# A gated mix of linear attention and a bilinear feed-forward block: the turn between two pairs of token chunks laid out step by step

## The chip, the core and the metric

The kernel runs on one core of a Trainium2 chip. It is judged by the device time of one execution in microseconds (us). The engines are named as in the profile: PE is the matrix engine (PEld its weight loads), DVE the vector engine, ACT the scalar engine, POOL the GpSimd engine, SP the engine that only issues DMAs here. Each takes its own instructions in the order in which the program was written (every compute helper of this kernel pins that order) and waits for the others by semaphores.

## What is computed

Input x has 2048 tokens of 512 features. The output mixes two branches per token, with g a sigmoid of a weighted sum of the token:

```python
g = _sigmoid((x * gate_w).sum(-1, keepdims=True))
a = _A_ref(x, A_wqkv, A_wo)            # linear attention, 32 heads of 16
b = _B_ref(x, B_w_gate, B_w_up, B_w_down)   # ((x W) * (x V)) W2, F = 1792
return g * a + (1 - g) * b
```

In the attention, phi(t) = t + 1 where t > 0, else exp(t), plus 1e-6; kv = sum of phi(k) v, z = sum of phi(k), and o = (phi(q) kv) / (phi(q) z + 1e-6), then o times wo. Nothing in it depends on the order of tokens.

## The kernel before

**Precision.** Every large product is done with operands split in two float32r parts, hi (a rounded copy, written by ACT, names ending in h) and lo (the rest, written by DVE with a subtraction, names ending in l), in three matmuls of 128x128 by 128x512: hi hi, hi lo, lo hi (`mm3`). So each operand that PE reads costs one ACT and one DVE instruction first: `hh`/`hl` for h = (xW)(xV), `oh`/`ol` for the attention's o, `wch`/`wcl` and `dh`/`dl` for weights, `xah`/`xal` and the like for x.

**Stages.** A first stage makes kv, z and the gates. Then the tokens are worked off in two *pairs* of two 512-token chunks each (c = 0 and 1). A pair has 16 *units*: two of kind q (q for half of the heads) and 14 of kind f (one 128-wide piece of W and V). A unit multiplies 2x2 blocks in the manner of Strassen: seven products, six matmuls each, in the order `UNIT`, accumulated in the PSUM banks bY, bX, bR and bS, with DVE's bR, t and bS between them: bR (in step 1) must be there for the product of step 3, t (step 3) for that of step 5, bS (step 4) for that of step 6. Each of the seven steps is a *slot*. Slots are numbered through, 7 per unit, 112 per pair, so that pair 0's last unit is slots 105 to 111. In a slot the program issues, in this order: the product, what is due from the slot before (`evacuate`), what is written for that slot in a table (`later(slot, fn)`), the unit's own step, and a *job* of three matmuls of the down projection, which lags by a group of two units and is also made of seven products; its sums are held in SBUF tiles M (`macc[i, d]`), the one of product 1 in PSUM (`pM`).

**The turn.** After a pair's last unit, `turn(pair)` closes the pair. 48 *pieces* of three matmuls make the outputs: 8 outputs (four row blocks d for c=1, then four for c=0) of 6 pieces, four with the operands `oh`, `ol` and two with those of h's last four blocks (`"12"`, `"22"` for c=1, `"11"`, `"21"` for c=0). When an output's pieces are done, DVE adds the bank to the M tile that holds that block of the down projection (`M<-M,pdn`), and it is stored. Pair 1 has all 48 pieces in its turn; of pair 0 30 are in the turn and 18 in the first 18 slots of pair 1. Until an output's sum, DVE has to

- gate h's last blocks with 1 - g (`c<-c,omg`) and split them (`plain`, through `hi_lo`);
- add M tiles to each other to get the blocks C12, C22, C21 and C11 (`add`, rows `M<-M` or `M<-M,pM`; 12 of them in the turn) and scale them with 1 - g (`scale`, rows `M<-M,omg`; 8 of them). In `ends` they stand as a list: sums of a block, then scales, two blocks after each other; `turn` takes two of the list per piece in the first five steps and one in each later;
- split o (`o_split`), c=1 in the last unit, c=0 in steps 18 to 21 of the turn;
- for pair 0, split pair 1's x (`x_split`, seven splits of 128x1024), whose parts are loaded in the last unit.

**q scaling.** In `attention`, the normaliser's reciprocal is stored and read back broadcast (`norm`, a DMA `rb<-den` on SP) and multiplied into q (`scale`, DVE `phq<-phq,rb`), four times for each of the two q units (j), three slots apart. `ZAT[j]` holds the slots, counted from that unit; its last number is the first `norm`, and `scale` follows six slots later.

**Buffers.** All 128x512 work tiles come from one pool of 45 (`get`, `put`) handed out in the order in which they were given back; the new owner waits for the last reader of the old.

Of the kernel before, what the change touches and what calls it, by code (L numbers as in the profile page):

```python
# [10 lines left out]
ALU = mybir.AluOpType  # L11
# [14 lines left out]
NPAIR = NC // 2  # L26
# [5 lines left out]
NG = NF // 2  # L32
# [4 lines left out]
UNIT = (2, 3, 4, 1, 5, 6, 7)  # L37
# [5 lines left out]
def gated_mix(ctx: ExitStack, tc, xt, xp, x, wqkv, wq, wq_add, wo, wgu, wgu_add, wdn, wdn_add, wdl, gate_w, out):  # L43
# [12 lines left out]
    def act(dst, src, func=AF.Copy, **kw):  # L56
        pin(nc.scalar.activation(dst, src, func, **kw))  # L57

    def tt(dst, a, b, op):
        pin(nc.vector.tensor_tensor(dst, a, b, op=op))  # L60
# [19 lines left out]
    def dma(dst, src):  # L80
        tc.keep_in_program_order(nc.sync.dma_start(dst, src))
# [42 lines left out]
    units = len(order)  # L124
# [61 lines left out]
    def get(name):  # L186
        k = spare.pop(0)
        w = p2.tile([P, CH], F32R, tag=f"w{k}", name=name)
        held[id(w)] = (k, w)
        return w  # L190

    def put(*ws):
        for w in ws:
            spare.append(held.pop(id(w))[0])

    def f32(w):
        return w.bitcast(F32)
# [12 lines left out]
    def later(slot, fn):  # L210
        at.setdefault(slot, []).append(fn)

    def do(table, slot):
        for fn in table.pop(slot, []):
            fn()
# [23 lines left out]
    for t in range(2 * CH // P):  # L239
        c, i = divmod(t, CH // P)  # L240
# [11 lines left out]
    for k in range(KT):  # L252
        raw = f32(raw_of[k])
        a = get("xlead")
# [151 lines left out]
    def gate():  # L406

        act(gcol, scol, AF.Exp, scale=-1.0)
        pin(nc.vector.tensor_scalar_add(gcol, gcol, 1.0))
        pin(nc.vector.reciprocal(gcol, gcol))  # L410
        pin(nc.vector.tensor_scalar(ocol, gcol, -1.0, 1.0, op0=ALU.mult, op1=ALU.add))
        turned = get("turned")
        rows = f32(turned)[:, 0:2 * NT]
        pin(nc.vector.transpose(rows, both))
        for a in range(0, P, 2 * NT):
            dma(gates[:, a:a + 2 * NT], rows[a:a + 2 * NT])
        put(gw)
        later(now_slot[0] + 8, lambda: put(turned))
# [18 lines left out]
    def hi_lo(src, keep, hi_at, lo_at, when):  # L437

        two = []

        def hi():
            two.append(get("hh"))
            act(two[0], f32(src()))

        def lo():
            two.append(get("hl"))
            tt(two[1], f32(src()), f32(two[0]), ALU.subtract)
            if not keep:
                put(src())

        when(hi_at, hi)
        when(lo_at, lo)
        return two
# [8 lines left out]
    def d_load(g):  # L462
        if g < NPAIR * NG:
            draw[g] = p2.tile([P, 7, 2 * P], F32, tag="dr", name="dr")
            if g % NG < NG - 1:
                dma(draw[g][:, 0:3], wdn[g % NG])
            else:
                dma(draw[g][:, 0:4], wdl)

    def d_add(g):  # L470
        if g < NPAIR * NG and g % NG < NG - 1:
            copies(draw[g])
            dma_add(draw[g][:, 2:7], wdn_add[g % NG])

    def d_high(g, part):
        a, b = (PLAIN if g % NG == NG - 1 else DRAW)[part]
        dcs[g, part] = [p2.tile([P, b - a, 2 * P], F32R, tag=f"d{part}{v}", name=f"d{v}", bufs=1 + part // 2)
                        for v in "hl"]
        act(dcs[g, part][0], draw[g][:, a:b])

    def d_low(g, part):
        a, b = (PLAIN if g % NG == NG - 1 else DRAW)[part]
        h, l = dcs[g, part]
        tt(l, draw[g][:, a:b], h.bitcast(F32), ALU.subtract)

    macc = {}
    half = {1: [0, 1, 2, 3], 0: [2, 3, 0, 1]}

    class Group:
# [44 lines left out]
        def when(self, off, fn):  # L534
            if off >= 14 and self.last:
                tail.setdefault((self.pair, off), []).append(fn)
            else:
                later(self.T + off, fn)

        def plain(self):  # L540

            g, pair, when, B = self.g, self.pair, self.when, self.B
            self.rows, self.ends = {}, []

            def row(c):
                self.rows[c] = get("omg")
                there = gates[NT:2 * NT].rearrange("(n t) p -> n (t p)", n=NC)[2 * pair + c:2 * pair + c + 1]
                dma(f32(self.rows[c]), there[:, None, :].to_broadcast([1, P, CH]))

            def gate(key, c):  # L550
                tt(f32(B[key]), f32(B[key]), f32(self.rows[c]), ALU.mult)

            for c in range(2):
                when(3, lambda c=c: row(c))
            for key, c, off in (("12", 1, 6), ("11", 0, 7), ("22", 1, 13), ("21", 0, 14)):
                when(off, lambda key=key, c=c: gate(key, c))
                self.ops[key] = hi_lo(lambda key=key: B[key], False, off + 1, off + 2, when)
            for part, off in (2, 4), (1, 8):
                when(off - 1, lambda part=part: d_high(g, part))
                when(off + 1, lambda part=part: d_low(g, part))  # L560
            when(11, lambda: d_load(g + 1))
            when(14, lambda: d_add(g + 1))

            def add(a, b, d, op, free):
                m = macc[b, d]
                tt(f32(macc[a, d]), f32(macc[a, d]), m if b == STAYS else f32(m), op)
                if free and b != STAYS:
                    put(macc.pop((b, d)))

            for off, a, b in (2, 6, 2), (6, 7, 5):  # L570
                for d in range(2):
                    when(off + d, lambda a=a, b=b, d=d: add(a, b, d, ALU.subtract, False))

            def scale(d, c):
                w = c_tile(d, c)
                tt(f32(w), f32(w), f32(self.rows[c]), ALU.mult)
                if d == half[c][-1]:
                    put(self.rows[c])

            scales = [lambda d=d, c=c: scale(d, c) for c in (1, 0) for d in half[c]]  # L580
            adds = [[lambda d=d, a=a, b=b: add(a, b, d, ALU.add, (a, b) in ((6, 3), (7, 1), (7, 4)))
                     for a, b in some for d in range(2)]
                    for some in (((5, 3),), ((6, 1), (6, 3)), ((2, 4),), ((7, 1), (7, 4)))]
            self.ends = []
            for n in range(4):
                self.ends += adds[n] + scales[2 * n:2 * n + 2]

        def seed(self, i, d):
            if not self.first and i != STAYS:
# [31 lines left out]
        def job_of(self, off):  # L621
            k = off - 11
            return (DOWN[k // 2], k % 2) if 0 <= k < 14 else None

    groups = [Group(g) for g in range(NPAIR * NG)]

    def at_slot(slot):
# [126 lines left out]
    def x_split(i):  # L754
        hi, lo = xc[i]
        act(hi, lo.bitcast(F32))
        tt(lo, lo.bitcast(F32), hi.bitcast(F32), ALU.subtract)
# [70 lines left out]
                    rows[pair, c][:, None, :].to_broadcast([2, 2 * HB, P]))  # L828

    phs = {}  # L830
    ZAT = ((15, (21, 23, 24), 26, 28), (24, (31, 33, 35), 37, 40))
    QORDER = [(1, 0), (0, 1), (1, 1), (0, 0)]

    def attention(pair, j, n):
# [55 lines left out]
        for (r, c), s in zip(QORDER, (8, 8, 10, 13) if j == 0 else (8, 9, 10, 13)):  # L890
            later(T + s, lambda r=r, c=c: z_part(r, c))
            later(T + s + 5, lambda: put(zs.pop(0)))
        loads, adds, rec, first = ZAT[j]
        for e in range(4):
# [12 lines left out]
    def o_split(b, c):  # L907
        hi, lo, o = get("oh"), get("ol"), phs.pop((b, c))
        act(hi, f32(o))
        tt(lo, f32(o), f32(hi), ALU.subtract)  # L910
        put(o)
        os_[b, c] = [hi, lo]
# [3 lines left out]
    def pieces(k):  # L916
        for fn in queue[:k]:
            fn()
        del queue[:k]
# [3 lines left out]
    def c_tile(d, c):  # L923
        return macc[CAT[d // 2, c], d % 2]
# [34 lines left out]

    def turn(pair):  # L960

        gr = groups[pair * NG + NG - 1]
        ends_jobs(pair)
        ready = []
        for k in range(TURN[pair]):
            pieces(1)
            do(tail, (pair, 14 + k))
            do(tail, (pair, 14 + k, "x"))
            for fn in gr.ends[:2 if k < 5 else 1]:
                fn()  # L970
            del gr.ends[:2 if k < 5 else 1]
            for fn in ready:
                fn()
            ready = waiting[:]
            waiting.clear()
        waiting.extend(ready)

    TURN = (30, 48)
    for k in range(18):
        FILL[7 * units + k] = 1  # L980
    for i, off in zip(UNIT, (36, 38, 40, 41, 42, 43)):
        tail.setdefault((0, off, "x"), []).append(lambda i=i: x_split(i))
    later(7 * units + 1, lambda: x_split(7))
    for p in range(NPAIR):
        for k, off in enumerate((32, 33, 34, 35)):
            tail.setdefault((p, off, "x"), []).append(lambda k=k: o_split(k, 0))

    for p in range(NPAIR):
        last = 7 * (units * (p + 1) - 1)
        for k, s in enumerate((0, 2, 4, 5)):  # L990
            later(last + s, lambda k=k: o_split(k, 1))
    later(14, g2_load)
    later(15, g_evac)
# [15 lines left out]
    for n, (pair, kind, m) in enumerate(order):  # L1009
        unit(n, attention(pair, m, n) if kind == "q" else None)  # L1010
        if (n + 1) % units == 0:
            turn(pair)
# [59 lines left out]
```

## Time and profile before

| | us |
|---|---|
| median of 3 runs (lowest to highest) | 604.53 (603.42 to 605.12) |
| profiled execution | 603.9 |
| its span | 602.2 |
| DVE busy, ACT busy | 499.0, 408.9 |
| DMA busy, mean of 16 engines, by the three busy queues | 33.4%, 29.2%, 0.2% of the span |
| last matmul's start, last DVE instruction's start | 597.63, 598.06 |

The span is the time from the first to the last instruction of the profiled execution; 1.7 us lie around it. A row of the timeline reads: start, duration, engine, line, operation, output<-inputs, shapes, count, and in brackets the engine's idle time before and what ended it. Lines are those of the kernel, and most of the instructions come from one of four helpers (L51 matmuls, L57 ACT, L60 and L63 DVE), so that they are told apart by their tiles. A wait row reads: engine, tile and line that waited, what it waited for, us in total, number of times, longest.

### The profile page before, as it was taken

To read this page: it belongs to the slowest core of one execution; us is meant where nothing else is said; L and a number is where in the kernel's file an instruction comes from. 1 tells how busy PE (TensorE), PEld (TensorE's weight loads), DVE (VectorE), ACT (ScalarE), POOL (GpSimd) and SP (SyncE) were. 2 spreads that over 40 slices of the span, in tenths; PEclk is the share of its full clock that TensorE was granted. 3 is DMA by queue.
4 is the path that set the end of the run, shared out by engine and by line. 5 is a ranking of instruction groups with operands and counts; after the bars stand their busy time and mean duration, and the time that the engine had idled before them with its cause. 6 is when DMAs were issued, how large, how long until landed. Compare 5 with 4: busy or idle time off the path is not lost.

```text
span 602.2 us, 7746 instructions
## 1 busy us (share of the span) xinstructions
PE 588.0 (98%) x2579; PEld 480.1 (80%) x2579; DVE 499.0 (83%) x809; ACT 408.9 (68%) x734; POOL 61.2 (10%) x79
## 2 busy tenths in 40 slices
PE   8999999999999999999998899999999999999997
PEld 6888888888778888888877688887888888888775
DVE  6869967776998999888989956969999989799881
ACT  3858857668877877777763754888686878776300
POOL 0041000010011212021000200201010101000000
PEclk9999999999999999999999999999999999999999
DMA  8589566695684989787686157847855656340011
GB/s 305 202 180 302 129 207 153 136 261 125 151 217 114 198 212 225 183 202 182 164 227 202 70 123 192 172 138 189 202 121 117 167 112 134 78 100 14 0 71 70
DMA packets 44185, 95.55 MB, mean 159 GB/s; under 512 B 4305, under 2 KB 13521, under 8 KB 44113
## 3 DMA queue, kind: packets, MB, share of 16 engines
q0 software_dynamic: 9856, 36.18, 33.4%
q1 hardware_dynamic: 34144, 58.62, 29.2%
q8 instruction: 20, 0.33, 0.2%
q10 hardware_dynamic: 144, 0.26, 0.1%
q14 instruction: 21, 0.16, 0.1%
HBM read 83.76 MB, written 12.34 MB: 160 GB/s over the span
## 4 chain that ended last, share of the span: by engine, by line
PE 82%; DVE 10%; ACT 4%; DMA 2%; issue 2%; DVEq 0%; ACTq 0%
PE pdn L51 20%; PE bR L51 13%; PE bY L51 13%; PE bX L51 12%; PE pk L51 7%; PE gt L51 7%; PE bS L51 6%; DVE M L60 5%; PE pM L51 2%; DMA dr<-in_wdn 2%; DVE c L60 1%; DVE ol L60 1%; DVE wcl L60 1%; PE pkv L51 1%; ACT wch L57 1%
## 5 line engine op out<-in xcount | busy, mean ns | idle before, releaser
L60 DVE TENSOR_TENSOR wcl<-wr,wch 128x512 fp32r<-128x512 f32 (+1 forms) x96 | 74.2, 774 | 2.7 <-ACT wch L57 2.7
L51 PE MATMUL pdn<-hl,dh 128*128 128x512 f32 x176 | 68.7, 390 | 2.6 <-DVE hl L60 2.6
L60 DVE TENSOR_TENSOR M<-M,pdn 128x512 f32<-128x512 f32 x76 | 51.9, 683 | 21.8 <-PE pdn L51 21.8
L51 PE MATMUL pdn<-hh,dh 128*128 128x512 f32 x176 | 68.6, 390 | 0.0
L51 PE MATMUL pdn<-hh,dl 128*128 128x512 f32 x176 | 68.5, 389 | 0.0
L57 ACT ACTIVATE wch<-wr 128x512 fp32r<-128x512 f32 (+1 forms) x96 | 66.8, 699 | 0.0
L57 ACT ACTIVATE M<-pdn 128x512 f32<-128x512 f32 x84 | 50.3, 599 | 15.5 <-PE pdn L51 12.6
L57 ACT ACTIVATE hh<-c 128x512 fp32r<-128x512 f32 x56 | 35.2, 629 | 31.5 <-DVE c L60 31.4
L84 POOL DMA_DIRECT2D wr<-in_wgu_add x28 | 24.2, 865 | 296.3 <-ACT wr L57 156.2
L51 PE MATMUL bX<-xbh,wch 128*128 128x512 f32 x128 | 49.8, 389 | 0.0
L51 PE MATMUL bX<-xbh,wcl 128*128 128x512 f32 x128 | 49.8, 389 | 0.0
L51 PE MATMUL bX<-xbl,wch 128*128 128x512 f32 x128 | 49.8, 389 | 0.0
L51 PEld LDWEIGHTS pdn<-hl,dh 128*128 128x128 f32 x176 | 33.0, 188 | 10.1 <-DVE hl L60 3.4
L60 DVE TENSOR_TENSOR hl<-c,hh 128x512 fp32r<-128x512 f32 x56 | 38.5, 687 | 1.5 <-ACT hh L57 1.4
L51 PEld LDWEIGHTS pdn<-hh,dh 128*128 128x128 f32 x176 | 33.0, 188 | 7.2 <-ACT pdn L57 0.3
L51 PEld LDWEIGHTS pdn<-hh,dl 128*128 128x128 f32 x176 | 33.0, 188 | 6.9
L57 ACT ACTIVATE c<-bX 128x512 f32<-128x512 f32 x28 | 16.8, 601 | 30.4 <-DVE bS L60 30.4
L57 ACT ACTIVATE wr<-wr 128x512 f32<-128x512 f32 x64 | 36.7, 625 | 0.8 <-DMA wr<-in_wgu 0.8
L57 ACT ACTIVATE pdn<-M 128x512 f32<-128x512 f32 x60 | 35.5, 592 | 0.0
L57 ACT ACTIVATE m<-bY 128x512 f32<-128x512 f32 x32 | 19.0, 594 | 19.5 <-PE bY L51 17.7
L60 DVE TENSOR_TENSOR dl<-dr,dh 128x512 fp32r<-128x512 f32 (+1 forms) x40 | 29.6, 766 | 1.9 <-ACT dh L57 1.8
L60 DVE TENSOR_TENSOR t<-bR,c 128x512 f32<-128x512 f32 x32 | 22.0, 686 | 10.3 <-PE bR L51 9.4
(186 smaller groups left out, 1592.2 us busy)
## 6 DMA issues: line engine op xcount, KB each, us to landing
wr<-in_wgu_add POOLq DMA_DIRECT2D x28, 640.0 KB, 6.9
wr<-in_wgu SPq DMA_DIRECT2D x28, 384.0 KB
dr<-in_wdn_add POOLq DMA_DIRECT2D x12, 640.0 KB, 8.5
dr<-in_wdn SPq DMA_DIRECT2D x12, 384.0 KB
xraw<-in_x SPq DMA_DIRECT2D x16, 256.0 KB
terms<-zq SPq DMA_DIRECT2D x16, 256.0 KB
zt<-terms SPq DMA_DIRECT2D x16, 256.0 KB
rb<-den SPq DMA_DIRECT2D x16, 256.0 KB
```

The source lines that it names most:

```text
L51: tc.keep_in_program_order(nc.tensor.matmul(*args, **kw))
L57: pin(nc.scalar.activation(dst, src, func, **kw))
L60: pin(nc.vector.tensor_tensor(dst, a, b, op=op))
L84: tc.keep_in_program_order(nc.gpsimd.dma_start(dst, src, accum_op=ALU.add))
```

## The change

- h's last blocks `"22"` and `"21"` are split one step earlier: their hi parts in the same step as their gates (13 and 14, counted as offsets of the last group; the turn begins at 14), and by the order in which the steps were entered, both stand ahead of the M sums.
- The list `ends` is gone. Each sum and scale has an offset of its own (`steps`): sum and scale of a block alternate, and each block's come shortly ahead of its output sum. For pair 0, offsets of 44 and more, which are the six instructions of C11 (two sums and a scale for either half), go into slots 3, 4, 6 and 7 of pair 1. For pair 1 all stay in the turn.
- Four of the seven x splits (for the products 1, 5, 6, 7, `UNIT[3:]`) go to slots 0, 1, 2 and 4 of pair 1; before, three of them were in the turn and that of 7 in slot 1. Each stands two or three slots ahead of its product.
- The o splits of c=1 move from steps 0, 2, 4, 5 of the last unit to -3, -1, 0, 2 (the first two into the unit before).
- The `norm` of the first q unit starts at its slot 52 and not 28, so the loads stand at 52, 55, 58, 61 and the scales at 58, 61, 64, 67.

```diff
@@ plain
-            for key, c, off in (("12", 1, 6), ("11", 0, 7), ("22", 1, 13), ("21", 0, 14)):
+            for key, c, off in (("12", 1, 6), ("11", 0, 7)):
                 when(off, lambda key=key, c=c: gate(key, c))
                 self.ops[key] = hi_lo(lambda key=key: B[key], False, off + 1, off + 2, when)
+            when(13, lambda: gate("22", 1))
+            self.ops["22"] = hi_lo(lambda: B["22"], False, 13, 14, when)
+            when(14, lambda: gate("21", 0))
+            self.ops["21"] = hi_lo(lambda: B["21"], False, 14, 15, when)
...
-            scales = [lambda d=d, c=c: scale(d, c) for c in (1, 0) for d in half[c]]
-            adds = [[lambda d=d, a=a, b=b: add(a, b, d, ALU.add, (a, b) in ((6, 3), (7, 1), (7, 4)))
-                     for a, b in some for d in range(2)]
-                    for some in (((5, 3),), ((6, 1), (6, 3)), ((2, 4),), ((7, 1), (7, 4)))]
-            self.ends = []
-            for n in range(4):
-                self.ends += adds[n] + scales[2 * n:2 * n + 2]
+            def steps(off, *fns):
+                for k, fn in enumerate(fns):
+                    if pair == NPAIR - 1 or off + k < 14 + TURN[0]:
+                        when(min(off + k, 13 + TURN[pair]), fn)
+                    else:
+                        later(7 * units * (pair + 1) + (off + k - 14 - TURN[0]) // 2, fn)
+
+            for d in range(2):
+                steps(15 + 2 * d, lambda d=d: add(5, 3, d, ALU.add, False), lambda d=d: scale(d, 1))
+            for d in range(2):
+                steps(20 + 3 * d, lambda d=d: add(6, 1, d, ALU.add, False), lambda d=d: add(6, 3, d, ALU.add, True),
+                      lambda d=d: scale(2 + d, 1))
+            for d in range(2):
+                steps(39 + 3 * d, lambda d=d: add(2, 4, d, ALU.add, False), lambda d=d: scale(2 + d, 0))
+            for d in range(2):
+                steps(50 + 6 * d, lambda d=d: add(7, 1, d, ALU.add, False), lambda d=d: add(7, 4, d, ALU.add, True),
+                      lambda d=d: scale(d, 0))
@@ attention
-    ZAT = ((15, (21, 23, 24), 26, 28), (24, (31, 33, 35), 37, 40))
+    ZAT = ((15, (21, 23, 24), 26, 52), (24, (31, 33, 35), 37, 40))
@@ turn
-            for fn in gr.ends[:2 if k < 5 else 1]:
-                fn()
-            del gr.ends[:2 if k < 5 else 1]
@@
-    for i, off in zip(UNIT, (36, 38, 40, 41, 42, 43)):
+    for i, off in zip(UNIT, (36, 38, 40)):
         tail.setdefault((0, off, "x"), []).append(lambda i=i: x_split(i))
-    later(7 * units + 1, lambda: x_split(7))
+    for i, s in zip(UNIT[3:], (0, 1, 2, 4)):
+        later(7 * units + s, lambda i=i: x_split(i))
...
-        for k, s in enumerate((0, 2, 4, 5)):
+        for k, s in enumerate((-3, -1, 0, 2)):
             later(last + s, lambda k=k: o_split(k, 1))
```

PE's instructions and their order are the same in both kernels. Three places on DVE show what moves. The first is the end of pair 0's last unit and the start of its turn; `c` are the blocks of h, `wcl` next unit's weights, `t` and `bS` the unit's own steps. Before:

```order
L60 TENSOR_TENSOR t<-bR,c_3147 128x512
L60 TENSOR_TENSOR ol<-phq,oh 128x512
L60 TENSOR_TENSOR wcl<-wr,wch 128x512
L60 TENSOR_TENSOR bS<-t,bX 128x512
L60 TENSOR_TENSOR ol<-phq,oh 128x512
L60 TENSOR_TENSOR wcl<-wr,wch 128x512
L60 TENSOR_TENSOR c_3189<-bR,c_3189 128x512
L60 TENSOR_TENSOR c_3189<-c_3189,omg 128x512
L60 TENSOR_TENSOR c_3147<-bS,c_3147 128x512
L60 TENSOR_TENSOR c_3147<-c_3147,omg 128x512
L60 TENSOR_TENSOR M<-M 128x512 x2
L60 TENSOR_TENSOR hl<-c_3189,hh 128x512
```

And of the change:

```order
L60 TENSOR_TENSOR t<-bR,c_3155 128x512
L60 TENSOR_TENSOR wcl<-wr,wch 128x512
L60 TENSOR_TENSOR bS<-t,bX 128x512
L60 TENSOR_TENSOR wcl<-wr,wch 128x512
L60 TENSOR_TENSOR c_3193<-bR,c_3193 128x512
L60 TENSOR_TENSOR c_3193<-c_3193,omg 128x512
L60 TENSOR_TENSOR c_3155<-bS,c_3155 128x512
L60 TENSOR_TENSOR hl<-c_3193,hh 128x512
L60 TENSOR_TENSOR c_3155<-c_3155,omg 128x512
L60 TENSOR_TENSOR hl<-c_3155,hh 128x512
```

Both `ol` left this stretch, and `hl` went ahead of the second gate and of the first M sums; the two `ol` are now among four that all stand ahead of this t.

The second place is where pair 0's turn ends and pair 1's first unit begins. `m` is what bR subtracts, `xal` to `xc6l` are the x splits. Before, from the third x split on:

```order
L60 TENSOR_TENSOR xc4l<-xc4l,xc4h 128x1024
L60 TENSOR_TENSOR xc1l<-xc1l,xc1h 128x1024
L60 TENSOR_TENSOR xbl<-xbl,xbh 128x1024
L60 TENSOR_TENSOR xc6l<-xc6l,xc6h 128x1024
L60 TENSOR_TENSOR M<-M,pdn 128x512
L60 TENSOR_TENSOR xal<-xal,xah 128x1024
L60 TENSOR_TENSOR bR<-bX,m_3389 128x512
L60 TENSOR_TENSOR t<-bR,c_3418 128x512
L63 SCALAR_TENSOR_TENSOR phq<-ex,phq 128x512
L60 TENSOR_TENSOR wcl<-wr,wch 128x768
L60 TENSOR_TENSOR bS<-t,bX 128x512
```

And of the change, from the fourth on:

```order
L60 TENSOR_TENSOR xc1l<-xc1l,xc1h 128x1024
L60 TENSOR_TENSOR xbl<-xbl,xbh 128x1024
L60 TENSOR_TENSOR bR<-bX,m_3379 128x512
L60 TENSOR_TENSOR xc6l<-xc6l,xc6h 128x1024
L60 TENSOR_TENSOR M<-M,pM 128x512
L60 TENSOR_TENSOR M<-M 128x512
L60 TENSOR_TENSOR t<-bR,c_3410 128x512
L63 SCALAR_TENSOR_TENSOR phq<-ex,phq 128x512
L60 TENSOR_TENSOR wcl<-wr,wch 128x768
L60 TENSOR_TENSOR M<-M,omg 128x512
L60 TENSOR_TENSOR xal<-xal,xah 128x1024
L60 TENSOR_TENSOR bS<-t,bX 128x512
```

bR passed two x splits; half of C11's sums and scale, and the last x split, now stand between bR and bS.

The third place is slot 58 of pair 0, where the first moved q scale arrives; `den` is the normaliser of the second q unit. Before:

```order
L60 TENSOR_TENSOR c_2006<-c_2006,c_1861 128x512
L875 RECIPROCAL den<-den 128x128
L60 TENSOR_TENSOR den<-den,g_896 128x128
L60 TENSOR_TENSOR hl<-c_1909,hh 128x512
L60 TENSOR_TENSOR wcl<-wr,wch 128x768
L60 TENSOR_TENSOR t<-bR,c_2155 128x512
```

And of the change:

```order
L60 TENSOR_TENSOR c_1994<-c_1994,c_1849 128x512
L63 SCALAR_TENSOR_TENSOR phq<-phq,rb 128x512
L890 RECIPROCAL den<-den 128x128
L60 TENSOR_TENSOR den<-den,g_896 128x128
L60 TENSOR_TENSOR hl<-c_1897,hh 128x512
L60 TENSOR_TENSOR wcl<-wr,wch 128x768
L60 TENSOR_TENSOR t<-bR,c_2150 128x512
```

One DVE instruction more stands ahead of t; the same holds in pair 1. On SP the four `rb<-den` loads of the first q unit went from slots 28 to 37 to slots 52 to 61, past the stores `terms<-zq` of the second q unit and past weight and x loads.

More of the change, by code (lines that the diff above doesn't have):

```diff
@@ L542, in plain @@
             g, pair, when, B = self.g, self.pair, self.when, self.B
-            self.rows, self.ends = {}, []
+            self.rows = {}
             def row(c):
@@ L623, in job_of @@
             return (DOWN[k // 2], k % 2) if 0 <= k < 14 else None
+    TURN = (30, 48)
     groups = [Group(g) for g in range(NPAIR * NG)]
@@ L960, in turn @@
     def turn(pair):
-        gr = groups[pair * NG + NG - 1]
         ends_jobs(pair)
@@ L976, in turn @@
         waiting.extend(ready)
-    TURN = (30, 48)
     for k in range(18):
         FILL[7 * units + k] = 1
-    for i, off in zip(UNIT, (36, 38, 40, 41, 42, 43)):
+    for i, off in zip(UNIT, (36, 38, 40)):
         tail.setdefault((0, off, "x"), []).append(lambda i=i: x_split(i))
-    later(7 * units + 1, lambda: x_split(7))
+    for i, s in zip(UNIT[3:], (0, 1, 2, 4)):
+        later(7 * units + s, lambda i=i: x_split(i))
     for p in range(NPAIR):
```

## The prediction

> **What bounds the kernel now.** First the page: the busy line. Then TensorE's (PE's) waits in the windows around the two turns, then the engines' rows in order of time.
>
> ```profile
> PE 588.0 (98%) x2579; PEld 480.1 (80%) x2579; DVE 499.0 (83%) x809; ACT 408.9 (68%) x734; POOL 61.2 (10%) x79
> ```
>
> PE is busy for 588.0 of 602.2 us, and the change leaves its 2579 matmuls and their order alone. So only PE's idle time can change, and all of it is 14.2 us with the start and the last store. The waits of PE from 300 to 350 us (turn of pair 0) come first, those from 545 us on (turn of pair 1) second:
>
> ```profile
> PE pdn L51 <- DVE hl L60: 1.6, 1, 1.6
> PE bR L51 <- DVE bR L60: 1.3, 1, 1.3
> PE pdn L51 <- DVE ol L60: 1.2, 2, 1.0
> PE bS L51 <- DVE bS L60: 0.8, 1, 0.8
> ```
>
> ```profile
> PE pdn L51 <- DVE hl L60: 1.0, 1, 1.0
> PE pdn L51 <- DVE ol L60: 0.2, 1, 0.2
> ```
>
> All six wait for VectorE (DVE): in the turns DVE is the late engine. What such a wait costs is read from PE's rows around the one of 0.8:
>
> ```profile
> 311.26 0.39 PE L51 MATMUL bR<-xc6l,wch 128*128 128x512 f32 x1
> 311.49 0.39 PE L51 MATMUL bR<-xc6h,wcl 128*128 128x512 f32 x1
> 312.68 0.47 PE L51 MATMUL bS<-xah,wch 128*128 128x512 f32 x1 [0.80 <-DVE bS L60]
> 312.99 0.40 PE L51 MATMUL bS<-xal,wch 128*128 128x512 f32 x1
> ```
>
> Unhindered matmuls start 0.23 apart (311.26 to 311.49), although each row lasts 0.39. Here 1.19 lie between two starts, so 0.96 are lost, and the one after comes 0.31 later, which loses 0.08 more. A wait of w therefore costs about w + 0.27 us at most. The four rows of pair 0 (five waits) are 4.9 us of waiting and 6.2 us lost; the two of pair 1 are 1.2 and 1.8.
>
> **Part 1, h's splits and the o splits.** These are DVE's rows in the last unit of pair 0, and then those of the turn's start:
>
> ```profile
> 308.80 0.68 DVE L60 TENSOR_TENSOR t<-bR,c 128x512 f32<-128x512 f32 x1
> 310.63 0.69 DVE L60 TENSOR_TENSOR ol<-phq,oh 128x512 fp32r<-128x512 f32 x1 [1.14 <-ACT oh L57]
> 311.24 0.68 DVE L60 TENSOR_TENSOR wcl<-wr,wch 128x512 fp32r<-128x512 f32 x1
> 311.84 0.69 DVE L60 TENSOR_TENSOR bS<-t,bX 128x512 f32<-128x512 f32 x1
> ...
> 314.93 0.69 DVE L60 TENSOR_TENSOR c<-bR,c 128x512 f32<-128x512 f32 x1
> 315.65 0.69 DVE L60 TENSOR_TENSOR c<-c,omg 128x512 f32<-128x512 f32 x1
> ...
> 317.58 1.29 DVE L60 TENSOR_TENSOR M<-M 128x512 f32<-128x512 f32 x2
> 318.79 0.68 DVE L60 TENSOR_TENSOR hl<-c,hh 128x512 fp32r<-128x512 f32 x1
> ```
>
> A DVE row costs 0.60 (311.24 to 311.84), or 0.72 if it reads what the row before wrote (314.93 to 315.65). Two `ol` (c=1) stand in front of bS and of the gates today and are waited for at 310.63; after the change they are three and one slots earlier than this unit, and the other two move up as well. Cost: in front of t stand four `ol` instead of two, so 2 x 0.60 = 1.2 us more, and DVE had no gap there to take it up. t would end at 308.80 + 0.68 + 1.2 = 310.7. Who waits:
>
> ```profile
> 304.93 0.69 DVE L60 TENSOR_TENSOR bR<-bX,m 128x512 f32<-128x512 f32 x1
> ```
>
> ```profile
> 306.96 0.39 PE L51 MATMUL bR<-xc1h,wch 128*128 128x512 f32 x1
> ...
> 310.36 0.39 PE L51 MATMUL bR<-xc6h,wch 128*128 128x512 f32 x1
> ```
>
> bR, 1.2 later, ends at 306.82 and just meets 306.96. t at 310.7 misses 310.36 by 0.4: a new stall of 0.5 with its restart. bS then follows t and one `wcl` at 311.2 to 311.9, and PE, which comes to it at 310.75 + 1.36 = 312.1, doesn't wait. So the loss of 1.04 at bS becomes 0.5: **0.5 gained**. From there on: `c<-bR` at 312.6, its gate at 313.3, ScalarE's `hh` from 314.0, then `hl` at 314.7 directly and not behind two M sums. PE starts the turn at 312.1 + 1.36 = 313.5 and asks for this `hl` in its sixth piece, after 5 x 0.68, at 316.9. The wait of 1.6 goes: **1.85 gained**. If `hl` had been held anyway by `hh`, only the two sums' 1.2 would.
>
> **Part 2, C11's sums and four x splits out of the turn.** DVE's rows at the end of the turn:
>
> ```profile
> 332.97 0.68 DVE L60 TENSOR_TENSOR ol<-phq,oh 128x512 fp32r<-128x512 f32 x1
> ...
> 343.99 1.22 DVE L60 TENSOR_TENSOR xal<-xal,xah 128x1024 fp32r<-128x1024 f32 x1
> 345.12 0.69 DVE L60 TENSOR_TENSOR bR<-bX,m 128x512 f32<-128x512 f32 x1
> ```
>
> Today all 20 M rows (12 us) stand ahead of the first `ol` of c=0, and all seven x splits (1.13 each, 343.99 to 345.12) ahead of the next pair's bR. After the change 10 M rows stand ahead of that `ol`: counted on from `hl` at 316.7, 10 rows and two output sums with some dependent pairs end at 325.0, where PE asks at 313.5 + 24 x 0.68 = 329.8. Both waits for `ol` go: **1.75 gained**.
>
> The moved rows are not saved; they stand in the first unit of pair 1, whose slot 0 starts at T = 313.5 + 30 x 0.68 = 333.9 on PE. I count DVE on: four `ol`, two splits, four M rows, the third split and the output sums end at T+1.6; two x splits to T+3.9; bR to T+4.6, asked for at T+6.1 (slot 3). Fine, the wait of 1.3 goes (1.6 lost today). Then a split, two M rows, t (from T+7.6, when its product is done), a `phq`, a `wcl` of 0.87, an M row, the split for x7, and bS from T+11.5 to T+12.2: asked for at T+12.2 (slot 6). That is a dead heat: 0 to 0.4 lost, I take 0.2: **1.4 gained**.
>
> In the Trainium skill, page "VectorE: DVE Perf Modes", section "The DRAIN you can't avoid", the next op waits for the pipe to empty whether or not a semaphore stands between, so that chained ops cost nothing extra. By it the nine dependent M rows, now alternating sum and scale, would cost 0.60 like any other and bS would win by about 1 us, for a sum better by 0.2; the 0.72 of the rows above speaks against it.
>
> The output sums and stores of pair 0 get no later, and the POOL stores with the weight accumulations queued behind them get earlier. Pair 1 has no next pair: its moved sums come 25 to 44 pieces into 48, and the last scale stands 3 pieces (2 us) before the last output sum, so the end stays. Its two waits go: **1.8 gained** (two shorter waits that the list doesn't show, against a miss of a few tenths at bR as above).
>
> **Part 3, q scaling 24 slots later.** Rows of PE, DVE and ScalarE (ACT) in slots 34 to 40, pair 0, and PE's of pair 1:
>
> ```profile
> 160.45 0.50 PE L51 MATMUL bY<-xc4h,wch 128*128 128x512 f32 x1 [0.98 <-ACT m L57]
> ...
> 166.92 0.50 PE L51 MATMUL bR<-xc6h,wch 128*128 128x512 f32 x1 [0.73 <-DVE t L60]
> ```
>
> ```profile
> 156.63 0.68 DVE L63 SCALAR_TENSOR_TENSOR phq<-phq,rb 128x512 f32<-128x512 f32 x1
> ```
>
> ```profile
> 158.55 0.63 ACT L57 ACTIVATE hh<-c 128x512 fp32r<-128x512 f32 x1 [1.17 <-DVE c L60]
> ```
>
> ```profile
> 412.67 0.50 PE L51 MATMUL bY<-xc4h,wch 128*128 128x512 f32 x1 [0.52 <-ACT m L57]
> ```
>
> m waits on ACT behind `hh`, that for DVE's c, that behind the scale at 156.63. Without it m comes 0.60 earlier, and 0.98 becomes 0.4. t has a second scale ahead of it, so 1.1 of its delay goes, 0.5 more than PE already gained: **1.1 in pair 0**; in pair 1 the 0.52 goes with a little behind it: **0.6**. Where the scales arrive, DVE and PE read:
>
> ```profile
> 209.95 0.69 DVE L60 TENSOR_TENSOR t<-bR,c 128x512 f32<-128x512 f32 x1
> ```
>
> ```profile
> 210.69 0.50 PE L51 MATMUL bR<-xc6h,wch 128*128 128x512 f32 x1
> ```
>
> PE takes t here 0.05 after it ends: no slack. The first scale stands in front of this t (behind it the reciprocal), so PE loses **0.6, twice 1.2** for both pairs. The other three come behind a point where DVE catches up, and I give them nothing; up to 0.6 each if that fails. The four `rb` loads go with them on SP, past weight and x loads.
>
> **Sum.** 0.5 + 1.85 + 1.75 + 1.4 + 1.8 + 1.7 - 1.2 = 7.8 us. The profiled execution took 603.9 (span 602.2 and 1.7 around), so 596.1; the median of the runs, 604.53, is 0.6 above it, and I forecast 604.53 - 7.8 = **596.7**.
>
> **Rivals.**
> - *The backlog only moves (0.20).* DVE's work isn't less, and each place above where I count a tie (bR and t in both last units, bS in slot 6) turns into a stall of 0.6 to 1.6. Against it: 10 M rows fewer ahead of `ol`. With 1.6 kept at the first unit and about 1 more per pair: a gain of 4 to 5, 599.5 to 600.5.
> - *The late scaling is free (0.12).* DVE meets slots 57 to 61 earlier, since its start there moves too; all turn stalls go. Then 6.2 + 2.2 + 1.7 = 10.1, 594.4.
> - *Slower (0.05).* SP takes its queue in order, and a late buffer for an `rb` holds the weight load behind it. The load of 198.63 is read by ACT's copy at 207.94:
>
> ```profile
> 198.63 0.33 SPq L81 DMA_DIRECT2D wr<-in_wgu  x1
> ```
>
> ```profile
> 207.94 1.14 ACT L57 ACTIVATE wr<-wr 128x512 f32<-128x512 f32 x2
> ```
>
>  9.3 us of slack, transfer included. Held 15 us or more, each pair loses 5 to 6, above the gain: about 607. For it: few buffers are free there. Against: their readers end in time.
> - *Nothing to be seen (0.06).* Gains and new stalls cancel to within 1.8 us: 603 to 606.
>
> The forecast has 0.57. A measurement tells about 0.3% (1.8 us) from no change. Faster by more: 0.57 + 0.20 + 0.12 = 0.89; same 0.06; slower 0.05. The range, 594.2 to 600.5, takes in the first two rivals and leaves out the other two.
>
> **What would show it.** In the new profile: no PE wait for `hl` or `ol` in the turns; no wait for bR in slot 3 of pair 1; a new PE wait for t of about 0.4 in pair 0's last unit and of 0.5 to 0.6 where 210.69 stood, in both pairs; PE busy still 588. I am wrong if PE waits over 1 us in slots 3 to 6 of pair 1, if `hl` still comes late, or if a weight load on SP leaves us waiting.

## The result

| | before | after |
|---|---|---|
| median (lowest to highest) | 604.29 us (603.42 to 605.12), 4 runs | 596.53 us (596.0 to 597.76), 4 runs |
| ratio of the times, 95% interval | | 0.9875 [0.9853, 0.9896] |
| profiled execution, its span | 603.9, 602.2 | 596.77, 594.7 |
| PE busy, and span less busy | 588.0, 14.2 | 585.7, 9.0 |
| PE's losses from slot 3 of pair 0 on | 12.7 | 6.1 |

The change made the kernel 7.8 us faster. The losses in the last line are read as the prediction reads them: wherever two matmuls start more than 0.23 apart, the rest counts as lost. They explain 6.6 us. Another 0.92 lies where the change has no instruction, in the stage ahead: the same matmul of slot 3 of pair 0's first unit starts sooner in this one execution. Before, and then after (start and duration in us):

```profile
121.01 0.40 PE L51 MATMUL bR<-xc1l,wch 128*128 128x512 f32 x1
```

```profile
120.09 0.40 PE L51 MATMUL bR<-xc1l,wch 128*128 128x512 f32 x1
```

In the traces of all runs here this row starts between 119.89 and 122.92. So below I also give the **rest** of each profiled execution, its span less that start: 481.2 before, 474.6 after. It holds all that the edits touch, and leaves out the scatter ahead of them.

PE's rows after the change, at the places the prediction named and at one that it did not:

```profile
209.86 0.50 PE L51 MATMUL pdn<-hh,dh 128*128 128x512 f32 x1 [1.82 <-ACT pdn L57]
311.08 0.50 PE L51 MATMUL bR<-xc6h,wch 128*128 128x512 f32 x1
346.73 0.47 PE L51 MATMUL bS<-xah,wch 128*128 128x512 f32 x1
455.30 0.50 PE L51 MATMUL bR<-xc6h,wch 128*128 128x512 f32 x1 [0.46 <-DVE t L60]
551.47 0.50 PE L51 MATMUL bR<-xc1h,wch 128*128 128x512 f32 x1
```

Of the seven waits of the turns (the six rows of the prediction's two lists) none is left. What remains there is 0.40 in slot 110 (311.08), 0.23 in slot 6 of pair 1 (346.73) and 0.28 in pair 1's last unit (551.47). In slot 61 of pair 1 PE waits for t, as foretold. But in pair 0 the largest wait of the whole trace stands at 209.86, and it is not for t: PE waits for ACT, which fills a job's bank from an M tile (the *seed*). Here is what ACT did, with SP's loads (SPq rows: an issue) ahead of it:

```profile
194.78 0.63 SPq L81 DMA_DIRECT2D rb<-den  x1
196.57 0.33 SPq L81 DMA_DIRECT2D wr<-in_wgu  x1
...
208.17 1.15 ACT L57 ACTIVATE wr<-wr 128x512 f32<-128x512 f32 x2 [1.58 <-DMA wr<-in_wgu]
209.23 0.58 ACT L57 ACTIVATE pdn<-M 128x512 f32<-128x512 f32 x1
```

ACT stood 1.58 us at the copy of a weight load, and the seed is queued behind that copy. The load took 11.6 us from issue (196.57) to use (208.17). Before, it was issued at 198.63 and read at 207.94 with no wait. Right ahead of it now stands one of the moved `rb` loads. Whether that is the cause, and what each part of the change is worth, the runs below tell.

### The profile page after: what moved, and what is told of

Its sections match the earlier page's. It is cut to its first block, busy times and chain, and to the rows that moved or that the text cites. A ratio compares the mean times of both kernels' runs of the same rounds, so it can differ in the third digit from the quotient of the medians.

```text
span 594.7 us, 7760 instructions
## 1 busy us (share of the span) xinstructions
PE 585.7 (98%) x2579; PEld 479.4 (81%) x2579; DVE 501.2 (84%) x809; ACT 408.7 (69%) x734; POOL 61.2 (10%) x79
## 4 chain that ended last, share of the span: by engine, by line
PE 85%; DVE 7%; ACT 3%; DMA 3%; issue 2%; DVEq 0%; ACTq 0%
PE pdn L51 24%; PE bR L51 12%; PE bY L51 12%; PE bX L51 12%; PE pk L51 7%; PE gt L51 7%; PE bS L51 6%; PE pM L51 3%; DMA wr<-in_wgu 2%; DVE wcl L60 1%; DVE M L60 1%; DVE c L60 1%; DVE hl L60 1%; DVE t L60 1%; PE pkv L51 1%
```

## The experiments

All runs, with the ratio to the kernel before on the same chip. The rest is read from one execution of each, the median from 4 to 12:

| run | median us | ratio, interval | rest |
|---|---|---|---|
| the change | 596.53 | 0.9875 [0.9853, 0.9896] | 474.6 |
| e1_scaling_back | 596.8 | 0.9879 [0.9861, 0.9897] | 474.5 |
| e2_scaling_alone | 605.69 | 1.002 [1.0007, 1.0033] | 482.2 |
| f1_one_load_later | 597.52 | 0.987 [0.985, 0.989] | 475.5 |
| z72_scaling_later | 597.24 | 0.9878 [0.986, 0.9896] | 476.0 |
| z78_scaling_later | 593.71 | 0.9823 [0.9806, 0.9841] | 471.6 |
| f3_later_still | 597.83 | 0.9899 [0.9878, 0.992] | 475.3 |
| e3_h_later | 601.91 | 0.9959 [0.9945, 0.9973] | 478.3 |
| g1_hh_ahead | 597.65 | 0.9887 [0.9865, 0.9909] | 474.4 |
| e4_o_back | 599.13 | 0.9911 [0.9896, 0.9926] | 475.7 |
| f2_h_and_o_back | 600.81 | 0.9937 [0.9918, 0.9956] | 477.3 |
| e5_sums_in_turn | 601.12 | 0.9939 [0.992, 0.9958] | 478.8 |
| e6_x_in_turn | 598.64 | 0.9904 [0.9887, 0.9921] | 475.5 |

**The scaling (part 3).** First undone in the changed kernel, then done alone in the kernel before:

```diff
-    ZAT = ((15, (21, 23, 24), 26, 52), (24, (31, 33, 35), 37, 40))
+    ZAT = ((15, (21, 23, 24), 26, 28), (24, (31, 33, 35), 37, 40))
```

> The changed kernel with the first q unit's scaling back at slot 28. By the prediction's part 3 (1.7 us gained at slots 34 to 40, 1.2 lost at slot 59) the time rises by 0.5, to 597.0. By the trace of the changed kernel the new stall of 1.8 us for the seed of pdn in slot 60 of pair 0 belongs to this part too, so that the part lost more (about 1.9 + 0.6 + 0.3) than it gained (1.8): then the time falls by about 0.9, to 595.6, the waits for m and t in slots 34 to 40 are back at 1.0 and 0.7, and the one for the seed is gone. If that stall is only a chance lateness of one transfer, it may stay and the time rises.

```diff
-    ZAT = ((15, (21, 23, 24), 26, 28), (24, (31, 33, 35), 37, 40))
+    ZAT = ((15, (21, 23, 24), 26, 52), (24, (31, 33, 35), 37, 40))
```

> The kernel before with the scaling moved to slot 52 and nothing else. By the prediction's part 3: 0.5 faster, 603.8. If the moved loads of rb are what makes the weight load late, the seed of pdn waits here too in slot 60 of pair 0 (1.5 to 2 us) and the kernel is 0.5 to 1 slower than before, about 605. If the late weight load came from something else in the change (the turn lies 130 us later, so little else is left), no wait for the seed is seen and the time is 603.8.

Undone, the seed's wait is gone and the old one for m is back:

```profile
160.56 0.50 PE L51 MATMUL bY<-xc4h,wch 128*128 128x512 f32 x1 [1.03 <-ACT m L57]
```

Alone in the kernel before, the seed is waited for too:

```profile
207.67 1.15 ACT L57 ACTIVATE wr<-wr 128x512 f32<-128x512 f32 x2 [0.69 <-DMA wr<-in_wgu]
...
209.37 0.50 PE L51 MATMUL pdn<-hh,dh 128*128 128x512 f32 x1 [0.93 <-ACT pdn L57]
```

So the stall belongs to this part. All eight traces here that have the four loads at slots 52 to 61 as in the change show this wait for the seed (0.93 to 1.82 us), and no other does. Alone, the part costs 1.0 us of the rest (time: 1.002, just outside of 1). Counted by places it is less: in both pairs together slots 34 to 40 gain 1.8 and the places from slot 59 on lose 2.1, so 0.3; the other 0.8 was lost in the turn, where the edit moves nothing. Undone in the changed kernel, it shortens the rest by 0.1 only; but that execution lost 0.7 at bS in slot 13 (140.88), ahead of any instruction that the edit moves, and counted by places it is the 0.9 of the second expectation. The median did not fall (596.8). So the part costs between 0.3 and 0.9 us in its own places, and the 0.5 us gain of the forecast is not there in either.

Is it the one `rb` load in front of the weight load? One DMA, moved one slot:

```diff
-            later(T + first + 3 * k, lambda r=r, c=c: norm(r, c))
+            later(T + first + 3 * k + (j == 0 and k == 1), lambda r=r, c=c: norm(r, c))
```

> The changed kernel with one DMA moved by one slot: the second load of rb of the first q unit is issued in slot 56 and not 55, so behind the weight load that came late and not in front of it; its scale stays in slot 61. If what stands ahead in SP's queue decides, the weight load lands about 1.1 us sooner (256 KB at the 230 to 260 GB/s that the DMA engines moved there), ACT's copy waits under 0.6 (1.58 in the changed kernel), PE for the seed under 0.9 (1.82), and the time is about 595.5. If the 16 DMA engines are simply full (share 0.95 to 1.09 from 196 to 208 us) and share their time among all transfers under way, the weight load lands as late as before and the time stays at 596.5.

```profile
197.52 0.33 SPq L81 DMA_DIRECT2D wr<-in_wgu  x1
197.94 0.63 SPq L81 DMA_DIRECT2D rb<-den  x1
...
207.43 1.14 ACT L57 ACTIVATE wr<-wr 128x512 f32<-128x512 f32 x2
...
228.36 1.16 ACT L57 ACTIVATE dr<-dr 128x512 f32<-128x512 f32 x2 [1.26 <-DMA dr<-in_wdn]
...
231.57 0.50 PE L51 MATMUL pdn<-hh,dh 128*128 128x512 f32 x1 [1.34 <-ACT pdn L57]
```

The weight load is in time (no wait at 207.43, at most 9.9 us after issue), so its place behind the `rb` load did make it late, as the first theory said. But 20 us later the same thing happens to the next weight, `dr`: its copy waits 1.26, and PE 1.34 for a seed behind it. So the time, 597.52, did not fall to the 595.5 of that theory (of the 0.9 by which the rest grew, 0.85 is the loss in slot 13 again, as in e1). The windows say why (per window: busy time of the engines, granted clock, share of the 16 DMA engines, GB/s), first the changed kernel, then e1:

```profile
core 0: us, PE busy (x) PEld busy (x) DVE busy (x) ACT busy (x) POOL busy (x), PEclk, DMA share, GB/s
192.00:196.00 4.00, 4.00 (x19) 3.33 (x18) 4.00 (x8) 3.65 (x8) 1.72 (x2) 1.00 0.85 189
196.00:200.00 4.00, 4.00 (x20) 3.30 (x19) 3.97 (x7) 2.70 (x5) 0.86 (x1) 1.00 0.97 199
200.00:204.00 4.00, 4.00 (x19) 3.32 (x18) 3.97 (x8) 2.87 (x6) 0.00 (x0) 1.00 1.09 260
```

```profile
192.00:196.00 4.00, 4.00 (x20) 3.30 (x19) 4.00 (x7) 3.82 (x8) 0.86 (x1) 1.00 0.39 115
196.00:200.00 4.00, 4.00 (x19) 3.33 (x18) 3.96 (x7) 3.68 (x8) 1.72 (x2) 1.00 0.94 166
```

The DMA engines are full from 196 us on in both (0.94 and more); with the scaling moved they fill 4 us sooner (0.85 against 0.39), and what is issued then lands later. As an estimate, a load of 256 KB is 1.0 us at the 260 GB/s of the third window, so the two `rb` loads ahead are about the 2.3 us by which the weight load took longer (11.6 against at most 9.3). The Trainium skill, page "DMA: Bandwidth & Descriptors", section "Issuing engines are not separate DMA queues", says that transfers started by different engines run on the same 16 DMA engines and interleave. The trace of the changed kernel agrees: from 196 to 208 us, when both POOL and SP issue, two queues take 74.3% and 25.9% of these engines' time.

Two later places for the four loads and scales (the last number of `ZAT[0]` is 72, then 78):

> The changed kernel with the first q unit's loads of rb from slot 72 on (72 to 81) and the scales from 78 on (78 to 87), clear of the reciprocal of the second q unit, of its scales, and of the weight load that came late. If the loads of rb at 52 and 55 made that weight load late, the wait of 1.8 us for the seed of pdn is gone and so is the one for t in slot 59 to 61 of both pairs: 2.4 us gained less what four scales cost in their new places (0 to 0.6 each pair), 594.2 to 595.0. If the load was late for another reason, the wait for the seed stays: 596 or more.

> The same as with 72, six slots later: loads of rb at 78 to 87, scales at 84 to 93. If only the place next to the second q unit and the late weight load mattered, it is as fast as with 72 (594.2 to 595.0). If what counts is the step of the unit in which a scale stands, the two differ by 0.5 or more.

From 72, the stall at slot 60 is gone and another, larger one has come in its place:

```profile
249.90 0.61 SPq L81 DMA_DIRECT2D rb<-den  x1
...
253.74 0.33 SPq L81 DMA_DIRECT2D wr<-in_wgu  x1
...
266.04 1.15 ACT L57 ACTIVATE wr<-wr 128x512 f32<-128x512 f32 x2 [3.03 <-DMA wr<-in_wgu]
...
267.73 0.80 PE L51 MATMUL pdn<-hh,dh 128*128 128x512 f32 x1 [2.53 <-ACT pdn L57]
```

From 78, two of the loads stand behind that weight load, and no seed is late:

```profile
253.14 0.33 SPq L81 DMA_DIRECT2D wr<-in_wgu  x1
...
254.11 8.48 SPq L81 DMA_DIRECT2D rb<-den  x2
...
263.22 1.17 ACT L57 ACTIVATE wr<-wr 128x512 f32<-128x512 f32 x2
```

Its rest is 3.0 us shorter than that of the change, its ratio of 0.9823 [0.9806, 0.9841] lies clear of 0.9875: **the fastest kernel here, 593.71 us**. The four scales cost PE nothing in their new place. Why 72 is late and 78 is not stays open. The order on SP alone does not tell them apart: in both, two `rb` loads are issued in the 12 us ahead of that weight load (at 244.65 and 249.90 from 72, at 241.81 and 249.09 from 78). From 72 the DMA engines were fuller from 244 to 252 us (shares of 0.89 and 0.67 in two windows, 0.62 and 0.56 from 78), but no run changes that alone.

An attempt at more, with scaling from 78:

```diff
-    ZAT = ((15, (21, 23, 24), 26, 52), (24, (31, 33, 35), 37, 40))
+    ZAT = ((15, (21, 23, 24), 26, 78), (24, (31, 33, 35), 37, 40))
...
-                steps(50 + 6 * d, lambda d=d: add(7, 1, d, ALU.add, False), lambda d=d: add(7, 4, d, ALU.add, True),
+                steps(56 + 6 * d, lambda d=d: add(7, 1, d, ALU.add, False), lambda d=d: add(7, 4, d, ALU.add, True),
...
-        for k, s in enumerate((-3, -1, 0, 2)):
+        for k, s in enumerate((-5, -3, -1, 1)):
```

> The changed kernel with the first q unit's loads of rb from slot 78 on (as in the run of that name, 593.7), and two small moves: the o splits of c=1 two steps earlier in the two slots where they stand in front of t (-5, -3, -1, 1), and C11's sums and scales in slots 6, 6, 7 and 9, 9, 10 of pair 1, behind bS of its first unit. The losses left in slot 110 (0.4) and in slot 6 of pair 1 (0.2) go: 593.1. If the moved steps only meet bR and t of the next unit, the losses reappear in slots 8 to 12 and the time stays at 593.7 or rises by up to 0.6.

It gained nothing: 597.83 where 593.1, or at most 594.3, was expected. In pair 1, whose turn has no later slots, a sum and the scale of one C11 block now come after that block's output sum and store. The output lacks them there, and DVE works on for 3.5 us behind the last matmul, which is most of the loss against scaling from 78 alone. Slot 6 of pair 1 and t in slot 110 lose nothing any more, but bR of pair 0's last unit was late instead (0.68 lost): one o split more stands ahead of it.

**h's splits and the o splits (part 1).** Each put back by itself, then both:

```diff
-            when(13, lambda: gate("22", 1))
-            self.ops["22"] = hi_lo(lambda: B["22"], False, 13, 14, when)
-            when(14, lambda: gate("21", 0))
-            self.ops["21"] = hi_lo(lambda: B["21"], False, 14, 15, when)
-            for key, c, off in (("12", 1, 6), ("11", 0, 7)):
+            for key, c, off in (("12", 1, 6), ("11", 0, 7), ("22", 1, 13), ("21", 0, 14)):
...
-                steps(15 + 2 * d, lambda d=d: add(5, 3, d, ALU.add, False), lambda d=d: scale(d, 1))
+                steps(14 + 2 * d, lambda d=d: add(5, 3, d, ALU.add, False), lambda d=d: scale(d, 1))
```

> The changed kernel with h's last blocks split as before (one step later, behind two M sums). If the parts add up as in the sum, the 1.85 us of pair 0 and about 1.2 of pair 1 come back as a wait for hl: 599.5. If h's splits and the earlier o splits do the same work twice (without the two ol in front, the gates come 2.3 us sooner, and hl then makes it even behind two sums), at most 0.3 per pair is lost: 596.5 to 597.1, with a wait for hl under 0.3.

```diff
-        for k, s in enumerate((-3, -1, 0, 2)):
+        for k, s in enumerate((0, 2, 4, 5)):
```

> The changed kernel with the o splits of c=1 back at steps 0, 2, 4 and 5 of the last unit. By the sum: the wait for bS in the last unit of pair 0 is back at 0.8 (1.04 lost), the one for t in slot 110 is gone (0.5), so 0.5 per pair and about 597.4. If h's splits alone carry the wait for hl, no wait for hl is seen in the turn. If they don't, it comes back with up to 1.6 and the time is 598.5 to 599.5.

> The changed kernel with both h's splits and the o splits of c=1 as before. With either of them alone put back, PE did not wait for hl. If the two remove the same wait twice, it is back here with about 1.6 us in pair 0 and 1.0 in pair 1, beside the 0.8 for bS in the last unit; with DVE held by the second hh behind ACT's copy of dr (5.9 us when only h was put back) the waits for bR and bS in pair 1's first unit come on top: 601 to 604. If hl is still not waited for, the wait of the kernel before hung on something else in the turn, and the time is 599 to 602.

One thing in the first edit is not as before: in e3, and so in f2, one M sum stands ahead of the first `hl`, where the kernel before has two.

In e4 PE waits for bS, in the last unit and in slot 6 of pair 1, and not for `hl`:

```profile
313.80 0.47 PE L51 MATMUL bS<-xah,wch 128*128 128x512 f32 x1 [0.80 <-DVE bS L60]
...
348.89 0.47 PE L51 MATMUL bS<-xah,wch 128*128 128x512 f32 x1 [0.53 <-DVE bS L60]
```

The expectation was 0.5 in each pair and 597.4. Pair 0 loses 1.3 more than in the change, since the second of these waits comes on top, and pair 1 nothing more; the rest grows by 1.1, the median (599.13) by 2.6. In e3 PE doesn't wait for `hl` either. With both back, it does, in pair 0 and in pair 1:

```profile
318.67 0.50 PE L51 MATMUL pdn<-hl,dh 128*128 128x512 f32 x1 [0.97 <-DVE hl L60]
...
564.07 0.50 PE L51 MATMUL pdn<-hl,dh 128*128 128x512 f32 x1 [0.37 <-DVE hl L60]
```

These waits are 0.61 us shorter than in the kernel before (1.58 and 0.98): the one M sum less. So the two edits remove the same wait, and against one M sum either is enough. Against two, the o splits would fall short in pair 0: in e3 the first `hl` ends at 318.67, 0.04 before PE reads it, and one more row of 0.60 would leave a wait of about 0.6 (an estimate). Yet e3 is the slowest of the three (rest 3.7 us longer than the change): neither of its theories had that in it. Rows of DVE, PE and ACT in its turn:

```profile
317.99 0.68 DVE L60 TENSOR_TENSOR hl<-c,hh 128x512 fp32r<-128x512 f32 x1
...
318.71 0.39 PE L51 MATMUL pdn<-hl,dh 128*128 128x512 f32 x1
...
323.48 1.15 ACT L57 ACTIVATE dr<-dr 128x512 f32<-128x512 f32 x2 [6.67 <-DMA dr<-in_wdn]
324.54 0.62 ACT L57 ACTIVATE hh<-c 128x512 fp32r<-128x512 f32 x1
...
325.19 0.69 DVE L60 TENSOR_TENSOR hl<-c,hh 128x512 fp32r<-128x512 f32 x1 [5.91 <-ACT hh L57]
...
345.58 0.50 PE L51 MATMUL bR<-xc1h,wch 128*128 128x512 f32 x1 [1.75 <-DVE bR L60]
```

The second `hh` is queued on ACT behind a copy of the next group's weights, which waits 6.67 us for its load. DVE, in order, stands 5.91 at the second `hl` with its sums behind it. PE has other pieces to do and pays later: small waits for an M tile (0.30) and an `ol` (0.22) in the turn, then 1.75 at bR, 20 us later, and 0.54 at bS. In f2 the same `hh` stands behind the same copy, but there the load was used 9.4 us after its issue (10.5 in e3), ACT waited 3.16 and DVE 2.40; so PE waited only 0.15 for bR and 0.52 for bS, and f2, at 600.81, came out below e3 and just below its expected 601 to 604. To test this alone, I moved that one ACT instruction; DVE, PE, POOL and SP have the order of e3:

```diff
-                self.ops[key] = hi_lo(lambda key=key: B[key], False, off + 1, off + 2, when)
+                self.ops[key] = hi_lo(lambda key=key: B[key], False, off + (key != "21"), off + 2, when)
```

> The same as the run with h's blocks split as before (601.9), but one instruction of ACT, the second hh, stands ahead of ACT's copy of dr and not behind it, in both pairs; the order of DVE, PE, POOL and SP is the same as there. If the 5.9 us that DVE stood there came from hh standing behind a copy that waits for the load of dr, the wait falls under 1 us, the waits for bR (1.75) and bS (0.5) in pair 1's first unit go, and the time is 596.5 to 597.5. If it is the place of hl behind the two M sums on DVE that costs, the waits stay and the time is 601 to 602.

```profile
318.24 0.63 ACT L57 ACTIVATE hh<-c 128x512 fp32r<-128x512 f32 x1 [0.69 <-DVE c L60]
...
319.93 0.68 DVE L60 TENSOR_TENSOR hl<-c,hh 128x512 fp32r<-128x512 f32 x1
...
324.44 1.15 ACT L57 ACTIVATE dr<-dr 128x512 f32<-128x512 f32 x2 [5.57 <-DMA dr<-in_wdn]
```

ACT's wait for the load is still there, but DVE no longer waits behind it, and the rest is 474.4, that of the change. The place of one instruction of 0.62 us was worth 3.9. (The median, 597.65, is a little above what I expected; its profiled execution reached slot 3 at 122.92, the latest of all.)

**C11's sums and the x splits (part 2).**

```diff
-                    if pair == NPAIR - 1 or off + k < 14 + TURN[0]:
+                    if True:
```

> The changed kernel with the six M instructions of C11 of pair 0 at the end of the turn and not in slots 3 to 7 of pair 1. In the changed kernel bR of pair 1's first unit ends 1.1 us before PE asks for it; six M rows (3.9 us) in front of it turn that into a wait of about 2.8 in slot 3, the 0.2 of slot 6 goes: about 599.1. If DVE has idle time in the turn that takes them up, no wait for bR is seen and the time stays at 596.5.

```diff
-    for i, off in zip(UNIT, (36, 38, 40)):
+    for i, off in zip(UNIT, (36, 38, 40, 41, 42, 43)):
...
-    for i, s in zip(UNIT[3:], (0, 1, 2, 4)):
-        later(7 * units + s, lambda i=i: x_split(i))
+    later(7 * units + 1, lambda: x_split(7))
```

> The changed kernel with the x splits as before (six in the turn, that of 7 in slot 1). Two more splits of 1.13 then stand in front of bR in slot 1 of pair 1, 2.3 us against a slack of 1.1: a wait for bR of about 1.1 in slot 3, 597.8. If the sums alone were what made bR late, no wait is seen and the time stays at 596.5 or falls by the 0.2 of slot 6.

PE's row of slot 3 of pair 1 in e5, then in e6:

```profile
343.87 0.50 PE L51 MATMUL bR<-xc1h,wch 128*128 128x512 f32 x1 [2.55 <-DVE bR L60]
```

```profile
342.03 0.50 PE L51 MATMUL bR<-xc1h,wch 128*128 128x512 f32 x1 [0.59 <-DVE bR L60]
```

Both parts matter, the sums more: 2.55 waited where I expected 2.8, and 0.59 where I expected 1.1. The rest grows by 4.2 and 0.8; the medians, 601.12 and 598.64, lie above the expected 599.1 and 597.8. In e5 1.4 of that is no waiting but a slower clock (last section).

## Why the prediction came out right, and where it did not

| part | predicted gain, us | in the two traces, us |
|---|---|---|
| pair 0's turn (parts 1 and 2) | 5.5 | 5.6 |
| pair 1's turn | 1.8 | 2.0 |
| scaling, slots 34 to 40 | 1.7 | 1.8 |
| scaling, where it went | -1.2 | -2.8 |
| sum | 7.8 | 6.6 |

- **Which engine is late.** Right: every wait of the turns was DVE's and went. A wait of w costs w + 0.26 at 209.86 (1.82 waited, 2.08 lost with the next row), as the rule said.
- **Part 1, t and bS in the last unit.** Right: 0.40 lost at t against 0.5 forecast, the wait for bS gone; e4 brings exactly that wait of 0.80 back.
- **Part 1, `hl`.** The wait went, but the reason was incomplete. I put it all down to the two M sums ahead of `hl`. The runs show that the earlier o splits alone would have done with one M sum left ahead of it (e3), and that in the changed kernel the earlier split of h is worth something else in pair 0, which the prediction did not consider: a place on ACT ahead of a copy that waits for a DMA (g1). I had asked for what is queued behind each instruction on DVE, not on ACT. In the kernel before, that place held DVE for 0.87 us only.
- **Part 2.** Right in mechanism and size. PE's slot 0 of pair 1 and DVE's rows in that unit:

```profile
334.33 0.39 PE L51 MATMUL bY<-xah,wch 128*128 128x512 f32 x1
...
338.62 0.69 DVE L60 TENSOR_TENSOR bR<-bX,m 128x512 f32<-128x512 f32 x1
...
342.08 0.69 DVE L60 TENSOR_TENSOR t<-bR,c 128x512 f32<-128x512 f32 x1
...
345.90 0.69 DVE L60 TENSOR_TENSOR bS<-t,bX 128x512 f32<-128x512 f32 x1
```

Counted from slot 0 (T = 334.33), bR ended at T+5.0 (4.6 forecast), t began at T+7.75 (7.6) and bS at T+11.6 (11.5). PE took bR 1.1 us after its end, and bS at 346.73, 0.14 after its end: the dead heat, 0.23 lost against 0.2.

- **The dependent rows.** In this trace a scale follows the sum that it reads after 0.72, and the next, independent sum follows after 0.61:

```profile
317.62 0.69 DVE L60 TENSOR_TENSOR M<-M 128x512 f32<-128x512 f32 x1
318.34 0.69 DVE L60 TENSOR_TENSOR M<-M,omg 128x512 f32<-128x512 f32 x1
318.95 0.69 DVE L60 TENSOR_TENSOR M<-M 128x512 f32<-128x512 f32 x1
```

By the rule of the Trainium skill ("VectorE: DVE Perf Modes", section "The DRAIN you can't avoid") as I read it there, they would be alike; the same section adds that a next operation that is not held starts earlier, which I had left out. The measurement decides, and the 0.2 us lost at bS are lost.

- **Part 3.** The gains are right, the price is the step that failed: "The four `rb` loads go with them on SP, past weight and x loads" was priced at nothing. They fill the DMA engines 4 us sooner, where x and weight transfers are under way, and use up the 9.3 us of slack of the very load that the rival "slower" named. So one of the prediction's own signs of being wrong, a weight load on SP that leaves PE waiting, came true. That rival's mechanism was another (SP was not held: the load was issued at 196.57, which is 198.63 less the 0.92 and the 1.14 that the program was ahead by then), and its price 2.1 and not 5 to 6, since only a copy and a seed stood behind it. In pair 1, with no x loads, only t is late: 0.73 against 0.6. From slot 78 on there is no price, and 593.7 is near the 594.4 of the rival "the late scaling is free"; but it takes another place, for at slots 59 to 61 the scales were not free.
- **The sum.** The forecast of 596.7 was met by 596.53, but the rows of the two traces give 6.6 and not 7.8; the two profiled executions differ by 7.1, the medians by 7.8. That the sum and the medians agree is in part luck: 0.9 us of the profiled difference is the shorter stage ahead, whose scatter (119.89 to 122.92 here) is larger than the error. PE busy was not the fixed 588 that I took it for: 585.7 here, and 585.0 to 588.7 in runs with the same matmuls.

What stays open: in e3, g1, e4, f2 and e6 the median lies 1.3 to 1.7 us further above the change than the rest does. The five executions of e3, 601.4 to 602.7, are 5.4 above it by their median; the rest has 3.7 of that, and in its profile slot 3 begins 2.1 later. None of these edits moves an instruction ahead of slot 3, and why that stage should be later there I can't tell.

## What to carry to other kernels

When an instruction is moved, look at every in-order queue it passes, and above all at those that hold a wait for a DMA: an instruction behind such a wait comes as late as the load, and can hold up its reader's whole engine. A load that is moved has no free place where the DMA engines are full: count the kilobytes issued ahead of the next load that somebody waits for, and if you put it behind that one, ask which load is late then (f1). And undo the parts of a change both one at a time and together, since two edits that remove the same wait look worthless one by one.

## What the runs showed of the hardware

In the two traces with a PE wait of 2.5 us, the granted clock was half for some 3 us after it. After the 2.55 in e5, windows of that kernel, with the columns as above:

```profile
344.00:345.20 1.20, 1.20 (x5) 0.97 (x6) 0.94 (x1) 0.45 (x1) 0.00 (x0) 0.82 0.51 38
345.20:348.20 3.00, 3.00 (x9) 2.33 (x8) 2.02 (x3) 0.00 (x0) 0.00 (x0) 0.50 0.94 188
348.20:352.00 3.80, 3.80 (x19) 3.09 (x18) 3.24 (x6) 1.89 (x4) 0.00 (x0) 1.00 0.00 0
```

The granted clock is 0.50 from 345.2 to 348.2, and matmuls start 0.43 apart instead of 0.23: 1.4 us more than the wait itself. After the 2.53 in z72 the clock is 0.52 from 267.6 to 271.1. After 1.82 in the changed kernel it stayed at 1.00. So the price of w + 0.27 held up to 1.8 us, and at 2.5 a wait cost over a microsecond more; where between the two this begins, no run here shows. The Trainium skill, page "TensorE: Matmul & The Clock Gate", section "Why this matters for your kernels", asks for no idle gaps above about 3 us between bursts of matmuls; here 2.5 us of idle time (matmul starts 2.9 apart) were enough.
